# Holding batch 1's input loads behind the last weight conversion, with planner durations and priorities redone

## The chip, the cores and the metric

The kernel runs on one core of a Trainium2 chip. The metric is the device time of one launch in microseconds; the kernel before takes 2090.18 us as the median of three runs (2088.63 to 2092.16).

## The reference, cut to what matters

The input x holds 8 batches of 3072 rows by 256 columns. A two-dimensional Fourier transform (rows, then columns) is taken of each batch and its real part kept. Two dense layers follow, on all 24576 rows:

```
X = fft(fft(x, axis=1), axis=2).real              # 8 x 3072 x 256
h = max(X @ w1, X @ w2, X @ w3);  y = h @ w_out   # 256 -> 768 -> 256
h = y @ w_in                                      # 256 -> 1024
solu = h * softmax(h);  ln = (solu - mean) / sqrt(var + 1e-6) * g_ln
out = ln @ w_out2                                 # 1024 -> 256
```

All weights arrive as 64-bit floats and x as 32-bit floats. The kernel computes in pairs of 16-bit halves (a high and a low part).

## The kernel before, in words

**Two kinds of work.** The weights are prepared once. Each of the 16 weight pieces is loaded as raw 64-bit words (`ld`, SyncE, into one of two `raw` buffers), its magnitude is taken by ScalarE (`ga`, L961), and four VectorE instructions build the 32-bit float (`gd`, L965, L966, L967, L969). The pieces are 768 elements wide (w3, w1, w2 and w_out) or 512 (w_in, then w_out2, whose four are keyed `f`; ("gd", "f", 3) is the last of all). After that come subtractions, small matmuls with the column transform, common power-of-two scales, and the split into halves. The last chain of the preparation is that of w_out2: gains, mean, subtraction on GpSimd, scale, split (`wfg`, `wfm`, `wfs`, `wfn`, `wfh`, `wfl`). When the whole preparation is over, `open` releases its memory to the second layer, and `mh`, `ml` and then the first layer-2 matmul `h` (L802) can follow.

**The stream of x.** Each batch has 4 chunks: a load (`xla`, L387, SyncE, 768 KB, one of two `xs` buffers), a pair sum (`xgh`, L394; on VectorE for batch 0, on GpSimd for all others), a sum and a difference (`xfly`, L433, two instructions, GpSimd), a square sum, a scale, a split (`xlo`, L453 on GpSimd, or L354 on VectorE for half of batch 0), and matmuls (`al`). A batch feeds 6 of the 48 row tiles s; tile s takes transposes `z`, matmuls `be`, layer 1 (`l1`, `rl`, `rh`, `rlo`, `m`), and layer 2 (`h`, `he`, `hv`, `vl`, `vt`, `o`) on 4 subtiles.

**What sets the order.** Nothing is scheduled at run time. A planner in Python (`Schedule.run`, L253) simulates all engines with a duration for each operation and emits each engine's instructions in the order of that simulation. `deps` tell it what must come first; among operations that can start it takes the one with the lowest due time `vt`, which is a base value plus an entry of `BIAS`. Each engine, and the queue of SyncE that issues all loads, then works through its list in order. The semaphores that hold on the chip come from the data that instructions share, not from `deps`: a dep between operations that share no tile changes the emitted order alone. So `deps` at L610 between a load of x and ("gd", "f", 3) leaves no wait of SyncE on VectorE in the program.

**Due times that matter here.** For batch 1 the base value of `xgh` and `xfly` is near 4, and their BIAS is -8.8 and 21.8; that of `rlo` is 97.5 on top of s. On GpSimd they come before `rlo` wherever both can start.

Of the kernel before, what the change touches and what calls it, by code (L numbers as in the profile page):

```python
# [20 lines left out]
NCH = NG // GC  # L21
# [16 lines left out]
BIAS = {("xla", 0): 6.642, ("xgh", 0): 10.341, ("xfly", 0): -9.394, ("xsq", 0): -0.709, ("xhi", 0): 6.403,  # L38
        ("xlo", 0): 17.171, ("al", 0): -2.445, ("ah", 0): -11.543, ("alo", 0): -8.31, ("xnm", 0): -8.319,
        ("et", 0): -11.353, ("eth", 0): -10.064, ("etl", 0): -10.524, ("xall", 0): -24.875, ("xsc", 0): -9.255,  # L40
        ("mu", 0): 3.3, ("xla", 1): 19.575, ("xgh", 1): -8.838, ("xfly", 1): 21.834, ("xsq", 1): 19.306,
        ("xnm", 1): -2.102, ("xhi", 1): 6.849, ("xlo", 1): 2.359, ("al", 1): -2.09, ("ah", 1): 26.235,
        ("alo", 1): -10.133, ("et", 1): -13.32, ("eth", 1): 3.942, ("etl", 1): -8.044, ("xall", 1): -1.555,
        ("xsc", 1): -25.218, ("mu", 1): 3.943, "xla": -20.985, "xgh": 16.273, "xfly": 95.893, "xsq": 148.589,
        "xnm": 34.632, "xhi": -119.918, "xlo": -89.65, "al": -59.029, "ah": -52.388, "alo": -87.057, "et": 0.242,
        "eth": -1.663, "etl": 3.014, "xall": -61.653, "xsc": -117.176, "mu": 56.199, ("zt", 0): -196.624,
# [27 lines left out]
        ("wcn", 1): -20.429, ("wne", 1): 6.325, ("wz", 1): -4.186, ("sub", 2): 7.956, ("wc", 2): 24.519,  # L74
        ("wce", 2): 24.431, ("am", 2): -1.999, ("wcn", 2): 11.089, ("wne", 2): 5.888, ("wz", 2): 1.956, ("amj",): 3.057,
        ("ws", "dg"): -5.917, ("ws", "all"): 1.262, ("ws", "pow"): -4.852, ("wsc", "part"): -14.198, ("wsc",): -1.52,
        ("whi", 1): -3.795, ("wlo", 1): -10.118, ("whi", 2): 23.432, ("wlo", 2): 6.478, ("wl1",): 1.684,
# [5 lines left out]
        ("os3", "dg"): 5.184, ("os3", "all"): 0.493, ("os3", "pow"): -17.762, ("scm", "part"): 12.326, ("scm",): 10.839,  # L83
        ("w3r",): -7.29, ("onm", 0): -0.103, ("ohi", 0): 2.169, ("olo", 0): 9.107, ("onm", 1): -0.381,
        ("ohi", 1): 8.157, ("olo", 1): -36.337, ("w3h",): -11.737, ("w3l",): 7.415, ("ld", "i"): -4.455,
        ("ga", "i"): 9.704, ("gd", "i"): 7.311, ("ami", 0): 4.584, ("wio", 0): -1.893, ("wih", 0): 22.616,
        ("wil", 0): -7.519, ("ami", 1): -0.805, ("wio", 1): 2.701, ("wih", 1): 0.766, ("wil", 1): 3.984,
        ("amij",): 9.396, ("is", "dg"): 13.68, ("is", "all"): 11.251, ("is", "pow"): -9.987, ("isc",): -11.798,
        ("win",): 0.578, ("gl",): -9.399, ("ld", "f"): 1.759, ("ga", "f"): -10.816, ("gd", "f"): -7.915,
        ("wfg", 0): -2.918, ("wfg", 1): 1.353, ("wfg", 2): -26.177, ("wfg", 3): -20.174, ("wfm",): -6.94,  # L90
        ("wfe",): 10.633, ("wfs", 0): 0.706, ("amf", 0): -6.053, ("wfs", 1): -24.272, ("amf", 1): 13.388,
        ("amfj",): 3.48, ("fs", "dg"): -1.106, ("fs", "all"): -5.106, ("fs", "pow"): -7.273, ("wfc", "part"): 9.879,
        ("wfc",): -13.035, ("wfn", 0): 3.542, ("wfh", 0): -6.144, ("wfl", 0): -4.219, ("wfn", 1): -11.469,
        ("wfh", 1): 3.372, ("wfl", 1): 8.053, ("wf",): 0.298, ("open",): -1.093}
# [210 lines left out]
def fft_moe_solu_kernel(ctx, tc, x, x_last, w1, w2, w3, w_out, w_in2, w_out2, g_ln, c_alpha, c_beta, c_w, c_eye, out):  # L305
# [6 lines left out]
    op = sch.op  # L312
# [238 lines left out]
    def is_special(s):  # L551
        return s % NSB == NSB - 1
# [54 lines left out]
    def x_ops(b, c):  # L607
        k = (b, c)
        v = max(NSB * b - 2.0, -1.2) + 0.09 * c
        op(("xla", *k), "SP", 2900, x_load, k, v - 0.5, deps=[("xla", b, c - 1)] if c else [("xla", b - 1, NCH - 1)] * (b > 0),  # L610
           take=["xs"], lag=2500)
        op(("xgh", *k), *(("Pool", 2450) if b else ("DVE", 1100)), x_pairs, (*k, pool if b else dve), v - 0.3, deps=[("xla", *k)])
        op(("xfly", *k), "Pool", 2450, x_fly, k, v - 0.2, deps=[("xgh", *k)], take=["uv"], give=["xs"])
# [440 lines left out]
    for i in (1, 2):  # L1054
# [3 lines left out]
        for a in range(2):  # L1058
            pop(("wc", i, a), "PE", 2900, w_dft, (i, a), v, take=["mh"[a]],
                deps=[("sub", i, 0), ("sub", i, 1), ("const",)] + [("wc", 1, e) for e in range(2) if i > 1])  # L1060
# [277 lines left out]
```

## Time and profile before

| | us |
|---|---|
| median of three runs | 2090.18 |
| the profiled execution | 2085.87 |
| its span, first to last instruction | 2084.1 |
| busy in the span: TensorE | 1976.3 |
| VectorE | 1787.0 |
| ScalarE | 1551.7 |
| GpSimd | 1406.0 |

The profiled execution has its own time, 1.8 us above its span. The engines' busy times are averages over two quite different stretches: the preparation, in which TensorE waits often and at a lower clock, and the long even part. In the profile, PE is TensorE, DVE VectorE, ACT ScalarE, POOL GpSimd, SP SyncE.

### The profile page before, as it was taken

The numbers are of one execution on the slowest core, as the hardware profiler recorded it, in microseconds if no ns is written. First come the engines' busy times: TensorE is split into PE (matmuls) and PEld (weight loads), VectorE is DVE, ScalarE is ACT, GpSimd is POOL, SyncE is SP. The second block draws the span as 40 slices with busy tenths as digits, with TensorE's granted clock in tenths as the row PEclk, the third lists the DMA queues.
The fourth block names the chain that finished last, engine by engine and source line by source line (L and its number), as shares of the span: only waits on it lengthen the run. The fifth ranks groups of instructions, "written<-read, shape, count | busy, mean of one in ns | idle before, by whom it ended". The sixth has DMA issues, their size and how long they took to land. (4 is left out here: it accounts for less than half of the span.)

```text
span 2084.1 us, 41702 instructions
## 1 busy us (share of the span) xinstructions
PE 1976.3 (95%) x15004; PEld 1353.8 (65%) x15004; DVE 1787.0 (86%) x4090; ACT 1551.7 (74%) x3037; POOL 1406.0 (67%) x1814
## 2 busy tenths in 40 slices
PE   4569999999999999999999999999999999999998
PEld 2346666676666666666766666666666666666666
DVE  6989889888888888888888898888888888888884
ACT  2578976777887778777887778877787777777775
POOL 3669975656976679665786668766675656665663
PEclk8669999999999999999999999999999999999999
DMA  7534643333453335523543334533343234233325
GB/s 215 149 75 83 116 82 72 67 67 77 95 114 74 65 78 115 102 57 67 108 102 77 67 77 97 98 77 61 79 75 81 56 73 87 62 80 73 66 48 122
DMA packets 472706, 178.87 MB, mean 86 GB/s; under 512 B 453577, under 2 KB 453802, under 8 KB 469290
## 3 DMA queue, kind: packets, MB, share of 16 engines
q1 hardware_dynamic: 472498, 176.20, 40.4%
q8 instruction: 117, 1.92, 0.4%
q14 instruction: 91, 0.75, 0.1%
HBM read 37.75 MB, written 25.17 MB: 30 GB/s over the span
## 5 line engine op out<-in xcount | busy, mean ns | idle before, releaser
L877 PE MATMUL omm<-wf,vt 128*128 128x256 f16 x4608 | 533.1, 273 | 6.0 <-DMA vt<-vh 5.3
L802 PE MATMUL h<-win,mo 128*128 128x512 f16 x2280 | 523.4, 379 | 2.3 <-DVE v L832 1.8
L877 PEld LDWEIGHTS <-vt 128*128 128x128 f16 x4608 | 450.3, 98 | 73.2 <-DMA vt<-vh 6.6
L680 PE MATMUL l<-pq,wl 128*128 128x256 f16 (+2 forms) x3456 | 453.3, 274 | 23.9 <-DVE sv L714 8.4
L728 POOL TENSOR_TENSOR rhl<-sv,rhl 128x512 f16<-128x512 f32 x288 | 336.8, 1175 | 196.5 <-ACT rhl L723 195.4
L863 POOL TENSOR_TENSOR vh<-v,vh 128x1024 f16<-128x1024 f32 x188 | 401.4, 2135 | 62.0 <-ACT vh L859 61.2
L680 PEld LDWEIGHTS <-wl 128*128 128x128 f16 x3456 | 332.2, 98 | 131.8 <-DVE sv L714 17.9
L738 PE MATMUL m<-rhl,wo 128*128 128x512 f16 x1728 | 413.7, 379 | 1.8 <-POOL rhl L728 1.0
L700 DVE SCALAR_TENSOR_TENSOR l<-ny,wn,l 128x256 f32<-128x256 f32 (+1 forms) x672 | 318.6, 481 | 111.1 <-ACT bs L351 110.3
L802 PEld LDWEIGHTS <-mo 128*128 128x128 f16 x2304 | 221.8, 98 | 249.0 <-DVE v L832 10.2
L351 ACT ACTIVATE bs<-l 128x256 f32<-128x256 f32 (+1 forms) x576 | 216.2, 379 | 158.1 <-PE l L680 138.6
L811 DVE TENSOR_REDUCE hst<-h 128x1 f32<-128x1024 f32 x190 | 231.6, 1219 | 50.8 <-PE h L802 49.8
L832 DVE SCALAR_TENSOR_TENSOR v<-h,hst,e 128x1024 f32<-128x1024 f32 x190 | 243.2, 1280 | 33.2 <-ACT e L826 25.3
L738 PEld LDWEIGHTS <-wo 128*128 128x128 f16 x1728 | 165.4, 99 | 154.0 <-issue 2.9
L837 ACT ACTIVATE jk<-v,hst 128x1024 f16<-128x1024 f32 x192 | 220.0, 1146 | 60.5 <-DVE v L832 59.0
L723 ACT CAST rhl<-sv 128x512 f16<-128x512 f32 x288 | 176.4, 613 | 112.7 <-DVE sv L719 96.4
L826 ACT ACTIVATE e<-h,hst,ms 128x1024 f32<-128x1024 f32 x190 | 228.9, 1205 | 6.3
L859 ACT CAST vh<-v 128x1024 f16<-128x1024 f32 x192 | 198.8, 1035 | 4.7 <-DMA vt<-vh 4.5
L850 POOL TENSOR_SCALAR hst<-hst,sc 128x1 f32<-128x1 f32 x192 | 66.0, 344 | 191.1 <-ACT jk L837 154.1
L719 DVE SCALAR_TENSOR_TENSOR sv<-l,sv 128x512 f32<-128x512 f32 x240 | 164.9, 687 | 3.6
L753 POOL TENSOR_TENSOR mo<-s,mw 128x512 f16<-128x512 f32 x96 | 121.5, 1281 | 12.3 <-ACT mw L351 8.1
L713 DVE SCALAR_TENSOR_TENSOR sv<-l,bs 128x256 f32<-128x256 f32 x288 | 120.5, 418 | 8.5 <-POOL rhl L728 0.6
(168 smaller groups left out, 2583.4 us busy)
## 6 DMA issues: line engine op xcount, KB each, us to landing
xs<-in_x_dram SPq DMA_DIRECT2D x32, 768.0 KB, 6.3
out_dram<-ob SPq DMA_DIRECT2D x96, 256.0 KB, 2.1
raw<-in_w_dram SPq DMA_DIRECT2D x6, 768.0 KB, 7.3
raw<-in_w_out_dram SPq DMA_DIRECT2D x14, 256.0 KB, 2.9
vt<-vh SPq DMA_TRANSPOSE x192, 4.3
raw<-in_w_in_dram SPq DMA_DIRECT2D x4, 512.0 KB, 4.5
cb<-in_c_beta_dram SPq DMA_DIRECT2D x1, 1553.0 KB, 12.9
z<-x SPq DMA_TRANSPOSE x48, 3.4
```

The source lines that it names most:

```text
L351: act.activation(dst, src, AF.Copy, scale=scale)
L680: mm(o, w_[w], hl[:, a, e, c0:c0 + n_], start=(n == 0), stop=(n == 2))
L700: dve.scalar_tensor_tensor(p[:, 0:WA], pq[s][1][:, 0:WA], w, p[:, 0:WA], ALU.mult, ALU.add)
L728: pool.tensor_tensor(t[:, 1], svs.pop((s, j, 0)), t[:, 0], ALU.subtract)
L738: mm(m[:, h], wo[:, w, j, hs], t[:, a], start=(j == 0 and n == 0), stop=(j == NJF - 1 and n == 2))
L802: mm(hp[:, f], m[:, a, d, ts_], win[:, w, d, fs], start=(n == 0), stop=(n == 5))
L811: dve.tensor_reduce(st[:, 0], y["h"], op=ALU.max, axis=AX.XY, negate=True)
L826: act.activation(y["e"], y["h"], AF.Exp, bias=st[:, 11], scale=ms_col(s, MS_T), accum_out=st[:, 3])
L832: dve.scalar_tensor_tensor(y["v"], y["h"], st[:, 2], y["e"], ALU.mult, ALU.mult, accum_out=st[:, 4])
L837: act.activation(new(hpool[0], "jk", [128, 2, 512], F16), y["v"], AF.Square, bias=st[:, 4], scale=-float(FF2), accum_out=st[:, 6])
L863: engine.tensor_tensor(y["vh"][:, 1], y["v"].rearrange("p a b -> p (a b)"), y["vh"][:, 0], ALU.subtract)
L877: mm(y["o"][:, 0:D], vt[:, a * 8 + c], wf[:, w, c], start=(n == 0), stop=(n == 23))
```

## The change

Batch 1's first load of x gets one more dep: the last weight conversion. (Its other chunks and the later batches follow it by the deps that were there.) Some durations that the planner uses are set higher, and all entries of BIAS are new numbers. The tiles, buffers, engines and arithmetic are the same; only the order of instructions on the engines and queues can differ.

```
-BIAS = {("xla", 0): 6.642, ..., ("xla", 1): 19.575, ("xgh", 1): -8.838, ("xfly", 1): 21.834, ... "rlo": 97.526, ...}
+BIAS = {("xla", 0): 3.913, ..., ("xla", 1): 18.196, ("xgh", 1): 5.745, ("xfly", 1): 26.145, ... "rlo": 68.905, ...}
...
-        op(("xla", *k), "SP", 2900, x_load, k, v - 0.5, deps=[("xla", b, c - 1)] if c else [("xla", b - 1, NCH - 1)] * (b > 0),
+        op(("xla", *k), "SP", 3500, x_load, k, v - 0.5, deps=[("xla", b, c - 1)] if c else [("xla", b - 1, NCH - 1)] * (b > 0) + [("gd", "f", 3)] * (b == 1),
...
-            op(("be", *k), "PE", (240, 480)[p], beta_mm, ...)
+            op(("be", *k), "PE", (264, 528)[p], beta_mm, ...)
...
-        op(("l1", *k), "PE", 658, l1_mm, ...)
+        op(("l1", *k), "PE", 663, l1_mm, ...)
...
-        slow, fast = 70 + 1.04 * n, 70 + 0.52 * n
+        slow, fast = 80 + 1.145 * n, 110 + 0.585 * n
...
-        pop(("ld", *key), "SP", 3.6 * n, f64_load, ...)
+        pop(("ld", *key), "SP", 4.4 * n, f64_load, ...)
...
-            pop(("wc", i, a), "PE", 2900, w_dft, ...)
+            pop(("wc", i, a), "PE", 4000, w_dft, ...)
...
-        pop(("wcn", i), "PE", 2340, w_dft_n, ...)
+        pop(("wcn", i), "PE", 3000, w_dft_n, ...)
```

## Rows read from the trace of the kernel before

**Rows 1.** Busy time by stretch (us from the start): engines, granted TensorE clock, DMA
```profile
0.00:57.00 57.00, 25.59 (x70) 15.45 (x70) 36.30 (x40) 18.45 (x30) 22.01 (x21) 0.88 0.75 222
57.00:132.00 75.00, 35.06 (x237) 26.90 (x238) 72.15 (x107) 44.44 (x88) 48.97 (x30) 0.58 0.52 134
132.00:162.00 30.00, 24.43 (x139) 15.79 (x138) 21.93 (x74) 27.73 (x50) 22.16 (x31) 0.91 0.03 6
162.00:200.00 38.00, 35.02 (x317) 23.48 (x315) 35.68 (x84) 31.15 (x65) 36.49 (x31) 1.00 0.39 77
200.00:2000.00 1800.00, 1782.07 (x13713) 1220.65 (x13711) 1571.51 (x3691) 1379.95 (x2719) 1241.31 (x1637) 1.00 0.40 80
2000.00:2084.00 84.00, 74.14 (x535) 51.58 (x533) 49.48 (x100) 49.94 (x90) 35.03 (x67) 0.99 0.47 98
```

**Rows 2.** Timeline of VectorE, TensorE, SyncE's queue: last conversion, first h, last raw load
```profile
130.28 1.46 DVE L969 SCALAR_TENSOR_TENSOR st<-raw,st 128x512 int32<-128x512 int32 x1
...
166.55 2.75 PE L802 MATMUL h<-win,mo 128*128 128x512 f16 x12
...
115.86 0.81 SPq L949 DMA_DIRECT2D raw<-in_w_out_dram  x2
```

**Rows 3.** VectorE's groups by form, 57 to 132 us: count | busy us, mean ns
```profile
L967 DVE SCALAR_TENSOR_TENSOR st<-raw,st 128x512 int32<-128x512 int32 x8 | 8.3, 1043 | 0.1
L969 DVE SCALAR_TENSOR_TENSOR st<-raw,st 128x512 int32<-128x512 int32 x8 | 8.1, 1019 | 0.0
L354 DVE SCALAR_TENSOR_TENSOR wl<-st,sc,wl 128x768 f16<-128x768 f32 x4 | 8.1, 2036 | 0.0
L965 DVE TENSOR_SCALAR st<-st 128x512 f32<-128x512 f32 x8 | 7.3, 918 | 0.3 <-ACT st L961 0.3
L966 DVE TENSOR_SCALAR st<-st 128x512 int32<-128x512 int32 x8 | 7.1, 883 | 0.1
L348 DVE TENSOR_SCALAR am<-am 128x2 int32<-128x2 int32 x1 | 5.1, 5094 | 0.0
...
L969 DVE SCALAR_TENSOR_TENSOR st<-raw,st 128x768 int32<-128x768 int32 x1 | 3.0, 2999 | 0.0
...
L348 DVE TENSOR_SCALAR am<-am 128x1 int32<-128x1 int32 x2 | 0.3, 148 | 0.0
```

**Rows 4.** VectorE's timeline, the same forms while GpSimd stood still
```profile
81.17 0.42 DVE L965 TENSOR_SCALAR st<-st 128x512 f32<-128x512 f32 x1
...
93.93 0.43 DVE L966 TENSOR_SCALAR st<-st 128x512 int32<-128x512 int32 x1
...
96.53 0.68 DVE L969 SCALAR_TENSOR_TENSOR st<-raw,st 128x512 int32<-128x512 int32 x1
...
77.77 1.01 DVE L354 SCALAR_TENSOR_TENSOR wl<-st,sc,wl 128x768 f16<-128x768 f32 x1
...
13.57 0.96 DVE L969 SCALAR_TENSOR_TENSOR st<-raw,st 128x768 int32<-128x768 int32 x1
```

**Rows 5.** Timeline of GpSimd (and of VectorE, last line) around 82 and 100 us
```profile
81.68 3.08 POOL L453 TENSOR_TENSOR uh<-uv,uh 96x1024 f16<-96x1024 f32 x1 [4.59 <-ACT uh L445]
...
100.58 2.47 POOL L433 TENSOR_TENSOR uv<-xs 96x512 f32<-96x512 f32 x2
103.02 2.33 POOL L394 TENSOR_TENSOR xs<-xs 97x1024 f32<-97x1024 f32 x1
...
100.28 5.09 DVE L348 TENSOR_SCALAR am<-am 128x2 int32<-128x2 int32 x1
```

**Rows 6.** GpSimd's instructions on the buffers of x (`xs`) by stretch
```profile
57.00:132.00 75.00, 34.36 (x17) 0.58 0.52 134
132.00:162.00 30.00, 0.00 (x0) 0.91 0.03 6
162.00:200.00 38.00, 9.73 (x6) 1.00 0.39 77
```

**Rows 7.** VectorE's groups by form, 300 to 1900 us
```profile
L719 DVE SCALAR_TENSOR_TENSOR sv<-l,sv 128x512 f32<-128x512 f32 x198 | 136.1, 687 | 3.2
...
L719 DVE SCALAR_TENSOR_TENSOR sv<-sw,sv 128x512 f32<-128x512 f32 x42 | 45.1, 1074 | 0.4
```

More of the change, by code (lines that the diff above doesn't have):

```diff
@@ L37 @@
 HOP = dict(PE=200, DVE=130, ACT=150, Pool=150, SP=60)
[L38 to L46, printed above, removed]
[27 rows of a table removed]
[L74 to L77, printed above, removed]
[5 rows of a table removed]
[L83 to L94, printed above, removed]
@@ new lines @@
+BIAS = {("xla", 0): 3.913, ("xgh", 0): 34.799, ("xfly", 0): -38.007, ("xsq", 0): 23.212, ("xhi", 0): 11.929,
+        ("xlo", 0): 23.876, ("al", 0): -18.632, ("ah", 0): -15.284, ("alo", 0): -0.968, ("xnm", 0): -32.17,
+        ("et", 0): -26.116, ("eth", 0): 6.781, ("etl", 0): -39.996, ("xall", 0): -19.961, ("xsc", 0): -35.177,
+        ("mu", 0): -37.967, ("xla", 1): 18.196, ("xgh", 1): 5.745, ("xfly", 1): 26.145, ("xsq", 1): -7.37,
+        ("xnm", 1): -26.645, ("xhi", 1): 18.119, ("xlo", 1): -12.788, ("al", 1): 0.024, ("ah", 1): -1.903,
+        ("alo", 1): -22.945, ("et", 1): -10.243, ("eth", 1): -0.308, ("etl", 1): 10.347, ("xall", 1): 3.52,
+        ("xsc", 1): -18.909, ("mu", 1): 8.834, "xla": -35.206, "xgh": 9.507, "xfly": 99.83, "xsq": 147.293,
+        "xnm": 31.691, "xhi": -116.418, "xlo": -86.305, "al": -61.683, "ah": -46.137, "alo": -92.537, "et": 0.016,
+        "eth": 2.854, "etl": 7.849, "xall": -51.5, "xsc": -118.594, "mu": 63.532, ("zt", 0): -203.637,
[24 rows of a table added]
+        ("const",): -23.518, ("eye",): 9.596, ("constb",): 5.976, ("ld", 0): -25.93, ("ga", 0): 34.626,
+        ("gd", 0): -11.561, ("ld", 1): -21.531, ("ga", 1): -7.482, ("gd", 1): 23.214, ("ld", 2): -6.687,
+        ("ga", 2): 16.553, ("gd", 2): 24.091, ("sub", 1): -12.102, ("wc", 1): 7.152, ("wce", 1): -1.677,
+        ("am", 1): 38.371, ("wcn", 1): -37.192, ("wne", 1): 33.251, ("wz", 1): 13.049, ("sub", 2): 49.742,
+        ("wc", 2): 11.471, ("wce", 2): 24.6, ("am", 2): 1.444, ("wcn", 2): -13.165, ("wne", 2): -9.829,
+        ("wz", 2): -2.18, ("amj",): 3.147, ("ws", "dg"): -1.65, ("ws", "all"): -11.251, ("ws", "pow"): 12.944,
+        ("wsc", "part"): -39.515, ("wsc",): 3.261, ("whi", 1): -2.03, ("wlo", 1): -0.692, ("whi", 2): 25.704,
[6 rows of a table added]
+        ("scm", "part"): 27.744, ("scm",): -5.484, ("w3r",): -1.376, ("onm", 0): -7.27, ("ohi", 0): -30.766,
+        ("olo", 0): 26.373, ("onm", 1): -11.059, ("ohi", 1): 3.742, ("olo", 1): -59.531, ("w3h",): -18.86,
+        ("w3l",): 28.542, ("ld", "i"): 20.066, ("ga", "i"): 23.016, ("gd", "i"): 3.272, ("ami", 0): 10.252,
+        ("wio", 0): 19.512, ("wih", 0): 45.094, ("wil", 0): -11.125, ("ami", 1): -5.753, ("wio", 1): 2.627,
+        ("wih", 1): 36.889, ("wil", 1): 5.236, ("amij",): 15.29, ("is", "dg"): 8.763, ("is", "all"): 35.379,
+        ("is", "pow"): -10.409, ("isc",): -21.646, ("win",): 6.927, ("gl",): 2.71, ("ld", "f"): 34.252,
+        ("ga", "f"): -14.274, ("gd", "f"): -16.632, ("wfg", 0): 17.273, ("wfg", 1): -2.77, ("wfg", 2): -50.255,
+        ("wfg", 3): -28.967, ("wfm",): -9.849, ("wfe",): 5.167, ("wfs", 0): -27.207, ("amf", 0): -41.7,
+        ("wfs", 1): -28.19, ("amf", 1): 6.448, ("amfj",): 9.143, ("fs", "dg"): -24.677, ("fs", "all"): -3.746,
+        ("fs", "pow"): 0.738, ("wfc", "part"): 35.922, ("wfc",): -17.908, ("wfn", 0): -7.146, ("wfh", 0): -14.354,
+        ("wfl", 0): -21.968, ("wfn", 1): -33.02, ("wfh", 1): 43.4, ("wfl", 1): 6.051, ("wf",): 8.178, ("open",): -3.712}
@@ L650, in fft_moe_solu_kernel @@
             before = [("be", s, 0)] if p else [("be", s - 1, 1)] if s else []
-            op(("be", *k), "PE", (240, 480)[p], beta_mm, k, v, deps=[("zt", s), ("constb",), *before] + [("etl", b)] * is_special(s),
+            op(("be", *k), "PE", (264, 528)[p], beta_mm, k, v, deps=[("zt", s), ("constb",), *before] + [("etl", b)] * is_special(s),
                take=["misc"] if p else ["misc", "pq"])
@@ L755, in l1_ops @@
     def l1_ops(k, v, deps):
-        op(("l1", *k), "PE", 658, l1_mm, k, v, deps=[("bl", k[0], 0), ("bl", k[0], 1)] + deps, take=["l1"])
+        op(("l1", *k), "PE", 663, l1_mm, k, v, deps=[("bl", k[0], 0), ("bl", k[0], 1)] + deps, take=["l1"])
         op(("l1b", *k), "ACT", 265, l1_b, k, v, deps=[("l1", *k)], take=["bs"])
@@ L973, in from_f64 @@
     def from_f64(key, srcs, dst, n, v, take=(), after=()):
-        pop(("ld", *key), "SP", 3.6 * n, f64_load, (key, srcs, n), v - 0.2, deps=after, take=["raw", *take], lag=2000)
+        pop(("ld", *key), "SP", 4.4 * n, f64_load, (key, srcs, n), v - 0.2, deps=after, take=["raw", *take], lag=2000)
         magnitude, parts = f64_parts(key, dst, n)
@@ L1058, in fft_moe_solu_kernel @@
         for a in range(2):
-            pop(("wc", i, a), "PE", 2900, w_dft, (i, a), v, take=["mh"[a]],
+            pop(("wc", i, a), "PE", 4000, w_dft, (i, a), v, take=["mh"[a]],
                 deps=[("sub", i, 0), ("sub", i, 1), ("const",)] + [("wc", 1, e) for e in range(2) if i > 1])
@@ L1063, in fft_moe_solu_kernel @@
             pop(("am", i, a), "DVE", 870, amax, (2 * i - 2 + a, lambda i=i, a=a: wrs[i, a]), v, deps=[("wce", i, a)])
-        pop(("wcn", i), "PE", 2340, w_dft_n, (i,), v, deps=[("wce", i, 1)], take=["misc"])
+        pop(("wcn", i), "PE", 3000, w_dft_n, (i,), v, deps=[("wce", i, 1)], take=["misc"])
         pop(("wne", i), "ACT", 56, w_evac_n, (i,), v, deps=[("wcn", i)], give=["misc"])
```

62 rows, old and new, of the table BIAS are left out of this document.

## The prediction, made before the kernel was run

> **What bounds the kernel now.** I read the busy times by stretch first [rows 1]. From 200 to 2000 us TensorE is busy 1782.07 of 1800, at full clock. So this part is bound by TensorE, its whole slack is 17.9 us, and the same matmuls run after the change. The last 84 us hold 9.9 us of TensorE's idle time. The first 200 us are another matter: TensorE is busy 25.6 + 35.1 + 24.4 + 35.0 = 120.1 us of 200, and from 57 to 132 us its granted clock is 0.58. A startup shorter by some amount moves everything behind it forward by as much, because what follows is a full TensorE.
>
> So I asked which engine fills the startup. From 57 to 132 us it is VectorE, 72.15 of 75 us; TensorE has 35, ScalarE 44, GpSimd 49 [rows 1]. The last conversion's last instruction ends at 130.28 + 1.46 = 131.7 us, and the first h matmul starts at 166.55 [rows 2]. From 132 to 162 us no engine is full (VectorE 21.9 of 30, GpSimd 22.2, ScalarE 27.7): this stage is a chain, the tail of w_out2's preparation beside layer 1 of the first row tiles.
>
> Next I asked whether VectorE's 72 us are work, by its groups by form [rows 3] against single instructions of the same form while GpSimd stood still [rows 4]. They are not: the same conversion step takes 0.9 to 1.0 us in the mean and 0.42 to 0.68 when alone. The clearest case is a two-element mask that starts at 100.28 and takes 5.09 us: GpSimd had started a pair of x instructions at 100.58 and another at 103.02, which ends at 103.02 + 2.33 = 105.35, and the mask ends at 105.37 [rows 5]. VectorE's instruction ends where GpSimd's run of instructions ends. GpSimd worked 34.36 us on x buffers in this stretch [rows 6], and all of it belongs to batches 1 and 2, since batch 0 takes its pair sums on VectorE and its last sums of the other kind are done before 57 us.
>
> **The change part by part.**
>
> The dep. It moves batch 1's loads, and with them their sums on GpSimd, in the planned order behind the last conversion; batch 2 goes behind batch 1. What leaves the stretch is the excess of VectorE's instructions. L967: 8 x (1043 - 680) ns = 2.9 us, taking L969's clean 0.68 for both. L969: 8 x (1019 - 680) = 2.7. L354 on wl: 4 x (2036 - 1010) = 4.1. L965: 8 x (918 - 420) = 4.0. L966: 8 x (883 - 430) = 3.6. The mask L348: 5094 - 148 = 4.9. The 768-wide L969: 2999 - 960 = 2.0. Sum 24.2 us [rows 3, 4]. Not all of it goes, as some of GpSimd's work in the stretch is not that of batches 1 and 2. Batch 0's split at 81.68 lasts 3.08 us and stays [rows 5]; a VectorE instruction behind it loses between nothing and 3.1 us, and I take 1.6. The last conversion step lies beside the weights' own subtractions and took 1.46 instead of 0.68 us [rows 2, 4]; I count 0.8 for it and as much for a neighbour, 1.6 in all. So 24.2 - 1.6 - 1.6 = 21.0 us go, with bounds 24.2 - 3.1 - 1.6 = 19.5 and 24.2.
>
> What is late next. VectorE stands still for 75 - 72.15 = 2.85 us of this stretch [rows 1]. With faster conversions the two raw buffers and ScalarE's step in front come nearer to the limit, so I double the idle time: 2.8 us are given back, with bounds 0 and 5.6. The last conversion would then end near 113.5 us instead of 131.7.
>
> What the moved work meets. A chunk takes GpSimd 9.73 / 2 = 4.9 us undisturbed (six instructions are two chunks) [rows 6], a batch 19.5 us. It now falls into the chain behind the conversions, where GpSimd also has the subtractions of the weights and of layer 1's halves. GpSimd is idle there for 30 - 22.16 = 7.8 us [rows 1]. If a whole batch had to go through before the first h, 19.5 - 7.8 = 11.7 us would be added to the chain; if the planner finds only gaps, nothing. Batch 1 isn't needed until row tile 6, so the lower bound is the nearer one: I take one chunk in front of something on the path, 4.9 us.
>
> Does this work disturb VectorE later? The instruction with one input in PSUM takes 687 ns; the same with both in SBUF takes 1074 [rows 7]. Only the special row tiles, one in six, have the slow form, so 6 instructions per batch: 6 x 0.39 = 2.3 us on an engine that has 228 us of slack in 1800 [rows 1]. I take 0, at most 2.3. The Trainium skill, SBUF — State Buffer, "Who interferes with whom", says that VectorE contends with GpSimd in its two-port modes or with two SBUF inputs, and that whichever starts first holds the shared ports for its whole instruction. By that rule the excess is exchanged, not removed, wherever x's sums meet such forms again; rows 7 show how few remain, so the sum by the rule would be 2.3 us worse at most.
>
> The durations. They change nothing on the chip by themselves. They let the planned order of the startup lie nearer to what happens: the new 110 + 0.585 x 512 = 410 and 80 + 1.145 x 512 = 666 ns are the clean 0.42 and 0.68 us [rows 4]. Gain or loss from this alone: bounded by TensorE's idle time between 132 and 200 us, 5.6 + 3.0 = 8.6 us [rows 1], in either direction; I take 0.
>
> The priorities. For the even part and the end they can win at most 17.9 and 9.9 us [rows 1], and lose as much if the new order is looser. l1 and be get durations up by 1% and 10%, which isn't much for an order to follow. I take 0, with 5 us either way for the range.
>
> SyncE's queue. Nothing waits on a semaphore for the conversion: the loads only stand further back. Behind them in the list are the transposes z and vt. The loads wait for free x buffers alone, which are long empty by then, so I cost this at 0; if a load did stand in front of a transpose, it would cost its own issue, under 1 us as for the raw loads [rows 2].
>
> Sum: 21.0 - 2.8 - 4.9 = 13.3 us less. The profiled execution would go from 2085.87 to 2072.6. The median of the runs shown is 4.3 us higher, at 2090.18, and on it I forecast 2076.9 us.
>
> **The rivals.**
>
> 1. The chain that remains eats the gain. The first h is held by the last preparation as well as by layer 1 of tile 0. If the 30 us stage grows by the full 11.7 us and the idle time by 5.6, then 21.0 - 17.3 = 3.7 us remain: 2086.5, hardly to be told from no change. For it: GpSimd has 36.49 of 38 us from 162 to 200 [rows 1]. Against it: TensorE was near full there all the same, and there is no hurry for batch 1.
>
> 2. It doesn't do what it says. Without a semaphore, SyncE issues a load of batch 1 as soon as the queue lets it. The last raw load goes out at 115.86, 16 us ahead of the last conversion's end [rows 2], so x's sums may still meet the last two conversions: two of the eight 512-wide ones, 2 x (0.36 + 0.34 + 0.50 + 0.45) = 3.3 us of the gain lost, and 2080 comes out. Against more than this: GpSimd's list is ordered too. This lies inside my range.
>
> 3. Slower: GpSimd becomes the bound of the ramp. By its due times x's sums go ahead of rlo. Were batches 1 and 2 both to pass before the first h is fed, that is 39 us, less 7.8 idle, less the 18.2 us (21.0 - 2.8) won ahead: 13 us later, 2103. It decides at the first h: later than 166.55 us, and the change loses. For it: the two batches have only been delayed, not spread. Against it: batch 2's sums need buffers that batch 1 frees late, and the planner counts these durations.
>
> 4. The even part loosens under the new priorities: TensorE's idle time there goes from 17.9 to 28 us and the result is 2087, about no change.
>
> 5. More comes out: the bounds at their best, 24.2 us, plus 5 of the 8.6 us in the ramp: 29 us, 2061.
>
> **How the numbers follow.** The forecast with rival 2 in it: 0.56, its own range 2068 to 2083 (giving back 0 or 11.7 instead of 4.9, conversion bounds, 5 us for the priorities, not all at once). Rival 1: 0.12. Rival 3: 0.14. Rival 4: 0.10. Rival 5: 0.08. A measurement can tell 0.2%, 4.2 us, from no change. Faster: 0.56 + 0.08, with a third each of rivals 1 and 4 (0.07): 0.71. Slower: 0.14 and a little of rival 4: 0.16. Same: 0.13. The range runs from 2062 to 2093: it leaves out most of rival 3 and half of rival 5, less than 2 in 10.
>
> **What would show it.** In the profile after: no x instruction of batch 1 on GpSimd before the last conversions; L965 to L969 of 512 near 0.42 and 0.68 us in the mean, and no mask of 5 us; the last conversion's end near 113 us; first h between 145 and 158 us; TensorE's idle time in the even part near 18 us. Wrong would be: clean conversions with a first h still near 166 (the chain was not VectorE's), or an early h with the gain lost behind 200 us (GpSimd or the priorities).

## The result, and the profile after

The changed kernel takes 2116.82 us (median; 2112.44 to 2118.45) against 2089.40 (2088.13 to 2092.16) of the kernel before in the same session: a ratio of 1.0128, 95% interval 1.0115 to 1.0140. It is 27 us slower, outside the range; I had forecast 13 us faster. The profiled execution took 2117.41 us, its span is 2115.6, which is 31.5 us above the span of before (the two profiled executions lie further apart than the medians).

First the startup, which is where I looked. VectorE's groups by form, 57 to 125 us of the changed kernel (count | busy us, mean ns | idle before), to be read against [rows 3]:

```profile
L969 DVE SCALAR_TENSOR_TENSOR st<-raw,st 128x512 int32<-128x512 int32 x8 | 6.3, 782 | 0.0
L965 DVE TENSOR_SCALAR st<-st 128x512 f32<-128x512 f32 x8 | 5.6, 699 | 2.6 <-ACT st L961 2.6
L967 DVE SCALAR_TENSOR_TENSOR st<-raw,st 128x512 int32<-128x512 int32 x8 | 5.5, 689 | 0.1
L966 DVE TENSOR_SCALAR st<-st 128x512 int32<-128x512 int32 x8 | 5.3, 664 | 0.1
L354 DVE SCALAR_TENSOR_TENSOR wl<-st,sc,wl 128x768 f16<-128x768 f32 x4 | 3.9, 1008 | 0.0
...
L348 DVE TENSOR_SCALAR am<-am 128x2 int32<-128x2 int32 x1 | 0.2, 163 | 0.0
```

The mask that took 5.09 us takes 0.16, the 768-wide halves 1.01 instead of 2.04. No x instruction of batch 1 or later stands beside the conversions any more, as it should be: the last of them ends at 122.4 us and GpSimd's first instruction on batch 1 starts at 126.80. The timelines of VectorE, TensorE and SyncE's queue answer to [rows 2]:

```profile
121.73 0.69 DVE L969 SCALAR_TENSOR_TENSOR st<-raw,st 128x512 int32<-128x512 int32 x1
...
158.09 3.86 PE L802 MATMUL h<-win,mo 128*128 128x512 f16 x12
...
109.22 0.43 SPq L387 DMA_DIRECT2D xs<-in_x_dram  x1
```

The last conversion ends at 122.4 us (131.7 before), the first h starts at 158.1 (166.55), batch 1's first load of x goes out at 109.2. So the first h comes 8.5 us earlier, and the kernel is still slower. The busy times by stretch (columns as in [rows 1]) show where that went:

```profile
0.00:57.00 57.00, 24.58 (x68) 14.66 (x68) 38.57 (x37) 16.96 (x27) 22.33 (x21) 0.88 0.67 211
57.00:132.00 75.00, 51.48 (x315) 37.56 (x316) 59.04 (x143) 52.88 (x106) 29.38 (x31) 0.66 0.38 92
132.00:162.00 30.00, 19.02 (x116) 10.83 (x115) 19.92 (x50) 18.29 (x36) 27.10 (x23) 0.83 0.21 53
162.00:200.00 38.00, 32.33 (x221) 20.48 (x222) 28.85 (x71) 29.96 (x53) 33.27 (x31) 0.96 0.42 94
200.00:2000.00 1800.00, 1760.92 (x13567) 1203.15 (x13567) 1546.20 (x3651) 1368.21 (x2693) 1238.05 (x1611) 1.00 0.39 80
2000.00:2115.60 115.60, 105.09 (x719) 70.57 (x717) 69.16 (x141) 68.90 (x125) 56.88 (x100) 0.97 0.43 89
```

Busy time alone misleads while the clock is low, so I multiply it by the granted clock, which gives the matmul work done in microseconds at full clock (the granted clock of a stretch is the mean over its two levels, 1.2 and 2.4 GHz, as a share of 2.4). From 57 to 132 us that is 51.48 x 0.66 = 34.0 against 35.06 x 0.58 = 20.3 before: 13.6 us ahead. From 132 to 200 it is 15.8 + 31.0 = 46.8 against 22.2 + 35.0 = 57.3: 10.4 of them are given back in 68 us. The same product from 200 to 300 us is 8.2 lower (TensorE busy 93.30 at 0.98, against 99.66 at 1.00). In the even part TensorE's idle time from 400 to 2000 us has doubled; before and after, columns as above:

```profile
400.00:2000.00 1600.00, 1584.42 (x12206) 1085.82 (x12205) 1395.56 (x3275) 1222.84 (x2408) 1094.62 (x1444) 1.00 0.39 79
```

```profile
400.00:2000.00 1600.00, 1567.61 (x12067) 1072.15 (x12066) 1375.49 (x3246) 1209.32 (x2382) 1082.15 (x1421) 1.00 0.39 79
```

15.6 us of idle time became 32.4, and after the longer gaps the clock falls too (0.97 from 1300 to 1400 us). By counts of the finished l, m, h and o matmuls the changed kernel is about 5 us behind at 400 us and 27 behind at 2000. So some 22 us are lost in the even part, and some 5 net in a startup that had been 13.6 ahead. The other 4 of the 31.5 us between the two spans lie behind 2000 us, where the granted clock is 0.97 against 0.99.

What the even part waits for shows in the waits of the changed kernel from 400 to 2000 us (us in total, times, longest), first ScalarE's, then those of SyncE's queue:

```profile
ACT vh L859 <- DMA vt<-vh: 84.9, 61, 3.0
```

```profile
SPq L868 <- PE omm L877: 960.5, 131, 16.8
```

Before, the first of these is not there at all, and the second is this:

```profile
SPq L868 <- PE omm L877: 208.6, 39, 17.8
```

A transposing DMA reads one of two vh buffers and fills one of three vt buffers, and a vt buffer is free only when its o matmul is through. If o comes late in the order, the transposes back up, vh stays full, and ScalarE, which works its list in order, stands before the next vh with the `bs` copies of layer 1 behind it.

And in the ramp, the timeline of the changed kernel around TensorE's longest gap there (start, us, engine, line, operation, tiles; in brackets the idle time before it and what ended it):

```profile
137.93 3.71 POOL L433 TENSOR_TENSOR uv<-xs 97x512 f32<-97x512 f32 x3
...
141.70 0.10 POOL L399 MEMSET xb<- 32x4 f32 x1
141.83 1.06 ACT L403 ACTIVATE zj<-uv 97x1024 bf16<-97x1024 f32 x1 [2.06 <-POOL xb L399]
...
142.88 0.64 ACT L351 ACTIVATE bs<-l 128x256 f32<-128x256 f32 x2
143.28 0.88 DVE L700 SCALAR_TENSOR_TENSOR l<-ny,wn,l 128x256 f32<-128x256 f32 x2 [3.53 <-ACT bs L351]
...
144.88 1.04 PE L680 MATMUL l<-pq,wl 128*128 128x256 f16 x4 [4.87 <-DVE sv L714]
```

Read from the bottom: TensorE waits 4.87 us for VectorE, VectorE 3.53 for ScalarE's `bs`, and `bs` stands behind the square of batch 1's x (L403), which waits for a small instruction of GpSimd (L399) that stands behind the sums of that x in GpSimd's list. Work that nobody needs until row tile 6 is in front of layer 1 on an engine that keeps its order.

### The profile page after: what moved, and what is told of

Its sections match the earlier page's. It is cut to its first block, busy times and chain, and to the rows that moved or that the text cites. A ratio compares the mean times of both kernels' runs of the same rounds, so it can differ in the third digit from the quotient of the medians.

```text
span 2115.6 us, 41733 instructions
## 1 busy us (share of the span) xinstructions
PE 1993.4 (94%) x15004; PEld 1357.3 (64%) x15004; DVE 1761.7 (83%) x4090; ACT 1555.2 (74%) x3037; POOL 1407.0 (67%) x1814
## 4 chain that ended last, share of the span: by engine, by line
PE 64%; DVE 16%; ACT 7%; DMA 5%; POOL 4%; issue 4%; SPq 0%; DVEq 0%; ACTq 0%; POOLq 0%
PE h L802 18%; PE omm L877 17%; PE l L680 14%; PE m L738 12%; DMA vt<-vh 3%; DVE v L832 2%; DVE hst L811 2%; DVE l L700 2%; DVE sv L719 2%; ACT e L826 1%; PE beta L569 1%; ACT bs L351 1%; POOL uh L453 1%; POOL vh L863 1%; DVE sv L714 1%
## 5 line engine op out<-in xcount | busy, mean ns | idle before, releaser
L877 PE MATMUL omm<-wf,vt 128*128 128x256 f16 x4608 | 536.5, 274 | 10.4 <-DMA vt<-vh 6.0
L802 PE MATMUL h<-win,mo 128*128 128x512 f16 x2280 | 526.3, 381 | 12.0 <-DVE v L832 11.8
L680 PE MATMUL l<-pq,wl 128*128 128x256 f16 (+2 forms) x3456 | 455.1, 275 | 40.2 <-DVE sv L714 18.3
L802 PEld LDWEIGHTS <-mo 128*128 128x128 f16 x2304 | 222.6, 98 | 261.5 <-DVE v L832 21.0
L351 ACT ACTIVATE bs<-l 128x256 f32<-128x256 f32 (+1 forms) x576 | 213.4, 379 | 121.2 <-PE l L680 112.7
L859 ACT CAST vh<-v 128x1024 f16<-128x1024 f32 x192 | 200.0, 1042 | 87.6 <-DMA vt<-vh 84.9
L753 POOL TENSOR_TENSOR mo<-s,mw 128x512 f16<-128x512 f32 x96 | 122.2, 1279 | 28.6 <-ACT mw L351 27.0
```

Of the source, the lines that this page charges most:

```text
L351: act.activation(dst, src, AF.Copy, scale=scale)
L680: mm(o, w_[w], hl[:, a, e, c0:c0 + n_], start=(n == 0), stop=(n == 2))
L802: mm(hp[:, f], m[:, a, d, ts_], win[:, w, d, fs], start=(n == 0), stop=(n == 5))
L877: mm(y["o"][:, 0:D], vt[:, a * 8 + c], wf[:, w, c], start=(n == 0), stop=(n == 23))
```

## The experiments

Thirteen kernels, each timed beside the kernel before, whose median lies between 2089.48 and 2089.75 us in these sessions; the ratios are to that. Where a run fixes the order, the planner's loop is replaced by a list of the same operations, and only the list differs; in those kernels all lines below the planner have numbers 38 lower (L802 is L764, L859 is L821).

```
     def run(self):
-        ...                      # picks the next operation by deps, durations and BIAS
+        for i in ORDER:          # a written-out list of the same operations
+            o = self.ops[keys[i]]
+            o.fn(*o.args)
```

| run | us | ratio, 95% interval | last conversion ends | first h | idle 400 to 2000 |
|---|---|---|---|---|---|
| before | 2089.40 | | 131.7 | 166.6 | 15.6 |
| the change | 2116.82 | 1.0115 to 1.0140 | 122.4 | 158.1 | 32.4 |
| e1 new start, old even part | 2096.18 | 1.0020 to 1.0044 | 121.2 | 157.1 | 16.9 |
| e2 old start, new even part | 2116.61 | 1.0118 to 1.0148 | 131.2 | 166.9 | 30.9 |
| e3 wait and durations | 2118.99 | 1.0126 to 1.0156 | 118.3 | 171.2 | 32.0 |
| e4 x later by 80 us | 2117.35 | 1.0121 to 1.0155 | 109.9 | 143.5 | 23.0 |
| e5 the change, 3 vh | 2105.05 | 1.0052 to 1.0086 | 121.9 | 157.7 | 20.0 |
| e6 wait alone | 2110.23 | 1.0082 to 1.0112 | 102.8 | 182.5 | 18.7 |
| e7 durations alone | 2112.06 | 1.0093 to 1.0123 | 142.8 | 183.1 | 20.9 |
| e8 x on VectorE | 2096.59 | 1.0019 to 1.0045 | 121.8 | 164.6 | 17.4 |
| e9 later x held back | 2081.86 | 0.9949 to 0.9978 | 121.6 | 157.2 | 18.3 |
| e10 new start, held back | 2101.68 | 1.0043 to 1.0073 | 122.1 | 156.1 | 21.4 |
| e11 priorities alone | 2172.70 | 1.0380 to 1.0411 | 133.7 | 182.1 | 58.3 |
| e12 hold alone | 2086.35 | 0.9975 to 0.9993 | 125.7 | 160.4 | 16.9 |
| e13 spread alone | 2089.26 | 0.9992 to 1.0010 | 125.1 | 160.4 | 17.0 |

The last column is the time in us for which TensorE is not busy from 400 to 2000 us. Times by stretch and idle times are from each run's profiled execution.

**Which stretch loses.** Theory A: the new order of the even part is looser and loses 22 of the 27 us. Theory B: x coming later disturbs the even part by itself.

e1 takes the change's order up to 300 us of the plan and the order of before from there:

```
-ORDER = order of before
+ORDER = [operations the change starts before 300 us] + [the others in the order of before]
```

> The changed kernel's order up to 300 us of the plan, the order of the kernel before from there on; the same instructions. Theory A (the new priorities make the order of the even part looser, 22 of the 27 us; the startup costs some 5): the even part's TensorE idle time is back near 16 us from 400 to 2000, and the time is about 2089 + 6 = 2095, between 2090 and 2100. Theory B (loading x later is itself what disturbs the even part, whatever the priorities): still above 2108.

e2 is the reverse, cut at 200 us:

```
+ORDER = [operations before starts before 200 us] + [the others in the order of the change]
```

> The mirror image: the order of the kernel before up to 200 us of the plan, the changed kernel's order from there on. Theory A: the startup is that of before and the even part has 30 us or more of TensorE idle time from 400 to 2000, 2107 to 2118 us. Theory B: x was loaded early, so the even part is as before, 2089 to 2096.

e1's row from 400 to 2000 us (columns as above):

```profile
400.00:2000.00 1600.00, 1583.11 (x12209) 1086.04 (x12207) 1394.18 (x3274) 1220.55 (x2405) 1092.01 (x1435) 1.00 0.39 80
```

and e2's:

```profile
400.00:2000.00 1600.00, 1569.08 (x12062) 1072.39 (x12061) 1375.21 (x3244) 1207.36 (x2380) 1079.03 (x1419) 1.00 0.38 79
```

With the old order behind it, the same start loses 6.7 us instead of 27 (2096.18), and TensorE's idle time is back at 16.9. With the old start and the new order behind it everything is lost again (2116.61, idle 30.9), and the waits at vh are there (83.6 us). Theory A holds: some 20 us are the order of the even part, some 7 the start. The two don't add exactly: with the old start, the new order from 200 us of the plan on costs the whole 27.

**Which edit makes the order loose.** e3 keeps the wait and the new durations, with the old priorities:

```
-BIAS = {new numbers}
+BIAS = {numbers of before}
```

> The changed kernel with the old BIAS: the new dep and the new durations stay. Theory A: the even part's idle time is that of before, near 16 us; the startup is ordered by priorities that were made for other durations and may lose up to 20 us: 2090 to 2110, and a first h later than the changed kernel's 158 us. Theory B: as slow as the changed kernel in the even part (30 us idle), 2110 or more in all.

It is as slow as the change (2118.99, idle 32.0), without the waits at vh (2.8 us, once). So the new priorities are not needed for a loose even part, which is not what A said, and the vh buffers are not the only way to one; what loosens this one was not found. The three edits then each by themselves: the wait,

```
-... [("xla", b - 1, NCH - 1)] * (b > 0)
+... [("xla", b - 1, NCH - 1)] * (b > 0) + [("gd", "f", 3)] * (b == 1)
```

> The added wait alone: the planner keeps the old durations and the old priorities. Theory A (any plan that is worked out anew from 100 us on has a looser even part than the one from before, whatever triggered it): TensorE idle in 400 to 2000 us 25 to 35 against 15.6 before, 2105 to 2125 us. Rival (the new durations or the new priorities loosen it): idle 15 to 18, and only the start counts, 2085 to 2100. The conversions should end at 113 to 123 us in either case.

the durations (70 + 1.04 n to 80 + 1.145 n, and the others of the diff),

> The new durations alone: old priorities, no added wait, so x of batch 1 is loaded at 52 to 81 us as before. Theory A: even part as loose as with the change, idle 25 to 35 us in 400 to 2000, and the conversions as slow as before (end at 128 to 136 us), so 2110 to 2130. Rival (durations that follow the trace do the plan good or nothing, as the prediction had it at 0): 2084 to 2094, idle 14 to 18.

and the priorities:

```
-BIAS = {numbers of before}
+BIAS = {new numbers}
```

> The new priorities alone, with the old durations and without the wait. Theory P (the tight vh buffers of the changed kernel come with the new priorities, since neither the wait nor the durations alone showed them): ScalarE's wait at vh for the transposing DMA over 50 us in the run, TensorE idle in 400 to 2000 us 27 to 34, 2105 to 2130. Rival (it takes the priorities together with the durations): idle 15 to 22 and that wait under 10 us; 2088 to 2110 by what its start does.

The wait alone leaves the even part nearly as it was (idle 18.7), and the durations add 5 us of idle time to it (20.9), where theory A asked for 25 to 35: in the form "any new plan is looser" it has fallen. Each still costs some 20 us, more than the rival theories allowed, and much of it in the start: by busy time times clock e6 is 19.5 us behind the kernel before at 400 us, e7 13.3. With the wait alone the conversions end at 102.8 us, 29 us earlier than before and earlier than I expected, and the first h comes 16 us later than before, because the total of batch 1's x stands in TensorE's own list in front of the chain (TensorE's timeline of e6):

```profile
148.16 0.59 PE L407 MATMUL total<-xb,unit 128*128 128x4 f32 x2 [20.00 <-ACT zj L403]
```

The priorities alone cost 83 us and are the loosest of all (row of e11 from 400 to 2000 us):

```profile
400.00:2000.00 1600.00, 1541.67 (x11777) 1053.15 (x11776) 1331.86 (x3174) 1186.33 (x2331) 1055.31 (x1394) 0.99 0.38 77
```

My expectation there named the vh buffers and was wrong in that: ScalarE's wait at them is 19.6 us, and the longest TensorE gaps are o matmuls that wait for their transposed tile (28.8 us in four gaps). The effects don't add: 21 + 23 + 83 us alone, 27 together. The new priorities do far worse with the old durations and without the wait (83 us) than with both (27). But the whole set is no better than the wait alone or the durations alone, and all four mixtures that were run, like the set itself, are slower than before.

**What the vh buffers are worth.** e5 is the change's order, with one number changed:

```
-                vh=2, vt=3, ob=2, ...
+                vh=3, vt=3, ob=2, ...
```

> The change's order to the instruction, but with three buffers for the fp16 pair of V (vh) instead of two. In the change's trace ScalarE waits 84.9 us (61 times) at the vh buffers for a transposing DMA, and the DMA queue waits 960 us for o matmuls that free the transposed buffers; neither wait is in the trace of before. Theory V (these waits are where the even part loses): with a third buffer the ScalarE wait falls under 20 us, TensorE's idle time in 400 to 2000 us falls from 32.4 to 17 to 22, and the time to 2100 to 2106 us. Rival (the waits are a sign of a late TensorE and not its cause; what idles it is the order in which VectorE and ScalarE serve it): the ScalarE wait falls, the idle time stays at 28 to 34, and the time at 2112 to 2119.

```profile
ACT vh L821 <- DMA vt<-vh: 0.5, 1, 0.5
```

```profile
400.00:2000.00 1600.00, 1579.99 (x12160) 1083.75 (x12159) 1383.87 (x3268) 1213.86 (x2391) 1087.76 (x1432) 1.00 0.39 79
```

The wait of 84.9 us is gone (first row, the waits of e5; second row, its stretch), idle time falls from 32.4 to 20.0 and the time by 11.8 us. SyncE's queue waits for the o matmuls as long as before the edit (949.7 us); the third buffer only keeps that from reaching ScalarE. So 12 of the some 20 to 22 us that the even part lost are this chain. What the rest is was not taken apart.

**Where the start's gain went.** e4 takes the order of before and moves only the x steps of batch 1 and later, those before 480 us of the plan, up to 80 us back:

> The order of the kernel before, in which nothing but the stream of x from batch 1 on (loads, sums, splits, alpha matmuls, z transposes) stands 80 us of the plan later, until it meets the old place again near 480 us. This is the dep's idea without new durations or priorities. The forecast's own step (contention with the conversions is worth 13 to 21 us at the end): 2068 to 2078, conversion steps of 512 near 0.42 and 0.68 us, first h near 148 us. Rival (the startup's length is not set by VectorE's conversions, or the gain is lost in the ramp): 2085 to 2095. Theory B: 2105 or more.

```profile
200.00:300.00 100.00, 88.63 (x694) 59.28 (x692) 73.18 (x179) 70.90 (x138) 71.05 (x75) 0.97 0.39 84
300.00:400.00 100.00, 86.36 (x623) 56.71 (x622) 78.24 (x182) 72.75 (x140) 70.70 (x102) 0.98 0.39 85
```

The first h comes at 143.5 us, 23 us earlier than before, and 25 us of TensorE's time are lost from 200 to 400 us (its rows above), where by the plan batch 1's steps now press against row tile 6; no run took that apart. Theory B has the time right (2105 or more) and not the place: from 600 to 2000 us, behind the moved steps, TensorE idles 13.4 us against 12.7 before. So the first h decides nothing by itself.

e8 puts the pair sums and the residuals of batch 1's x on VectorE, with the change's planner, and the order of before from 250 us:

```
-... (("Pool", 2450) if b else ("DVE", 1100)), x_pairs, (*k, pool if b else dve)
+... (("Pool", 2450) if b > 1 else ("DVE", 1100)), x_pairs, (*k, pool if b > 1 else dve)
...
-            pool.tensor_tensor(t[:, 1], xuv.pop((b, c)), t[:, 0], ALU.subtract)
+            (dve if b == 1 else pool).tensor_tensor(t[:, 1], xuv.pop((b, c)), t[:, 0], ALU.subtract)
```

> The change with two of the four GpSimd steps of batch 1's x (the pair sums and the residuals, 18 of its 36 us of GpSimd work) on VectorE, planned with the change's numbers; from 250 us of the plan on, the order of before. Theory (after the change GpSimd is the bound of the ramp, 15.7 of 18 and 23.0 of 25 us in 132 to 175 us, because batch 1's x now stands among rlo, wfs and wfl): first h at 150 to 160 us, TensorE busy in 132 to 162 us over 22 (19.0 with the change), and 2082 to 2094 us, that is 3 to 14 under the 2096.2 of the change's start with the old order behind it. Rival (the ramp loses by TensorE's low clock and by the split of VectorE, which gets 9 us more work): 2093 to 2100.

2096.59, no better than e1; the first h goes to 164.6, and GpSimd fills up with other x (29.55 us on x's buffers from 132 to 200 us against 26.51 in e1). That points to whose x it is. GpSimd's busy time on x's buffers by stretch shows 52.5 us from 132 to 300 us in the changed kernel, more than two batches, where [rows 6] and the same view of before to 300 us have 29.2:

```profile
132.00:162.00 30.00, 14.13 (x9) 0.83 0.21 53
162.00:200.00 38.00, 11.49 (x9) 0.96 0.42 94
200.00:300.00 100.00, 26.84 (x17) 0.98 0.52 113
```

From 57 to 300 us it is 54.8 us (34 instructions) in the changed kernel and 63.6 (35) in the kernel before, and a batch is 12 such instructions, 19.5 us by the prediction's count: both work on x of batches 2 and 3 in the first 300 us, as soon as buffers allow, though batch 2 is first needed for row tile 12. e9 holds that back in the order of before and spreads batch 1's chunks:

```
 ORDER = order of before
+  x steps of batches 2 to 4 (loads, sums, squares, splits): 280 us and later, before 103 to 260
+  x steps of batch 1: the same sequence, further apart
```

> The order of before, neither the change's wait nor its numbers, with one thing moved: the early steps of x for batches 2 to 4, which the kernel before does at 103 to 260 us on GpSimd, are held back to 280 us and later, and batch 1's chunks are spread further apart; the other steps keep their order. Theory H (what disturbs the start is that x of batches that aren't needed for hundreds of us takes GpSimd, first beside the conversions, then in the ramp; batch 1 alone fits): last conversion ends at 116 to 124 us (131.7 before), first h at 150 to 160, TensorE busy in 132 to 200 us over 61 (59.4 before, 51.4 with the change), even part as before (idle 14 to 19 in 400 to 2000), 2072 to 2084 us. Rival B (moving x to a later place costs as much as it brings, as when batch 1 was moved by 80 us): TensorE idle grows in 300 to 500 us instead, and 2088 to 2105.

```profile
57.00:132.00 75.00, 43.42 (x276) 33.52 (x277) 64.09 (x118) 54.66 (x108) 41.73 (x33) 0.64 0.43 105
132.00:162.00 30.00, 23.71 (x163) 14.49 (x162) 26.19 (x80) 22.72 (x42) 23.09 (x27) 0.94 0.00 1
162.00:200.00 38.00, 37.62 (x342) 25.98 (x341) 36.12 (x86) 32.83 (x67) 25.98 (x27) 1.00 0.29 56
200.00:300.00 100.00, 99.91 (x737) 67.89 (x735) 85.47 (x202) 73.53 (x146) 65.43 (x81) 1.00 0.49 96
300.00:400.00 100.00, 95.09 (x713) 63.83 (x714) 89.49 (x214) 76.80 (x152) 80.94 (x108) 1.00 0.47 95
```

2081.86 us: the first version that beats both kernels, by 7.9 us against before. Theory H holds for its times (last conversion 121.6, first h 157.2, TensorE 61.3 us busy from 132 to 200), and TensorE stays full from 200 to 300 us, where the change lost 6.7. Some 3 us are paid back from 300 to 400, where the held x now lies.

The two moves apart, and the same hold behind the change's start:

> The run that beat both kernels (2081.9 us) moved two things in the order of before. Here the early x of batches 2 to 4 alone is held back to 280 us and later; batch 1's steps stand as before. Theory H2 (x of the later batches is most of it: it leaves GpSimd at 103 to 121 us beside the conversions, and altogether in 160 to 280 us): last conversion ends at 124 to 128 us, first h at 160 to 164, and 2083 to 2087 us. Rival S (batch 1's chunks were the ones in the way, the later batches sat in gaps): last conversion 129 to 132, first h 165 to 168, 2087 to 2092.

> The other half: batch 1's chunks are spread as in the run with 2081.9 us, and x of batches 2 to 4 comes as early as before. Theory H2: last conversion 126 to 131 us, first h 161 to 167, 2086 to 2091 us. Rival S: last conversion 119 to 124, first h 155 to 160, 2080 to 2085.

> The change's start (as in the run that put the old order behind it, 2096.2 us), with x of batches 2 to 4 held back to 240 us and later, and the order of before behind 300 us of the plan. Theory H: GpSimd's x work in 132 to 300 us falls from 52 to under 35 us, and the time to 2084 to 2092. Rival C (batch 1 by itself is too late behind the last conversion: its square on ScalarE and its sums stand in front of layer 1 in the ramp): TensorE busy in 132 to 200 us stays at 50 to 53, and 2093 to 2100.

The hold alone wins 3.2 us (interval 0.07 to 0.25%), the spread alone nothing that can be told. Both bring the first h to 160.4, 6 us earlier than before. From 162 to 200 us they part (first row the hold alone, second the spread alone):

```profile
162.00:200.00 38.00, 37.27 (x317) 25.24 (x316) 35.61 (x83) 29.15 (x57) 24.20 (x28) 0.99 0.31 50
162.00:200.00 38.00, 34.63 (x273) 21.91 (x271) 31.34 (x74) 28.87 (x56) 33.58 (x29) 0.91 0.37 77
```

With the hold, TensorE's work there (busy by clock) is 37.27 x 0.99 = 36.9; with the spread alone it is 34.63 x 0.91 = 31.5, and the early h is given back. GpSimd works 9.73 us on x there with the spread alone and none with the hold, which is the likely reason. Together the two win 7.9, more than the sum, so theory H2, by which the hold is most of the gain, has the times of each half about right and not the share. Behind the change's start the hold takes GpSimd's x work from 132 to 300 us down to 27.7 us, as expected, and gains nothing: 2101.68, 5.5 above e1, of which 4.5 are idle time in the even part (21.4 against 16.9). TensorE is busy 53.2 us from 132 to 200, about what rival C expected. Its list also has some of batch 1's own steps in other places than e1's (its squares and scalings on ScalarE, some up to 40 places later), so this is not a test of the later batches alone. It speaks against them as what the change's start suffers from, and for batch 1 itself behind the conversions, in the lists of ScalarE and GpSimd, as in the gap before 144.88 us. That is a reading of the trace; no run took batch 1 out of that place alone.

## Why the prediction was wrong, point by point

- **The reading of the startup** held: VectorE's conversions were slowed by GpSimd, and mostly clean once x had gone. Of the 24.2 us that I summed for the seven groups, 5.0 remain (L965 8 x 0.28, L966 8 x 0.23, L969 8 x 0.10, L967 0.1), so 19.2 went; I had taken 21.0 with 19.5 as the lower bound.
- **What is late next** was mis-sized. Up to the last conversion's end VectorE is busy 54.58 of 65.4 us, so it idles 10.8 us where it had idled 2.85: 8.0 given back, not 2.8, and outside the bound of 5.6. Some 2 us of other work also moved in front of it, as VectorE's busy time up to there fell by 17.3 us and not by 19.2. The conversion ended at 122.4 instead of 113.5.
- **What the moved work meets**: I put one chunk, 4.9 us, on the path, with 11.7 as the bound. The path lost more than the 13.6 us of work won ahead: at 400 us the sum of busy time by clock is 3.9 us below before. I priced x by GpSimd's idle time. But the price was paid in the lists of ScalarE (the square in front of `bs`) and, in e6, of TensorE (its total, 20 us). And where TensorE has gaps, its clock stays down: 0.83 from 132 to 162 us against 0.91, the h matmul at 158.09 taking 3.86 us against 2.75.
- **Later disturbance of VectorE** I took as 0, at most 2.3 us. Means agree: the two-SBUF form takes 1109 ns (42 of them) against 1074. A single one is another matter; in the changed kernel:

```profile
1547.47 2.96 DVE L719 SCALAR_TENSOR_TENSOR sv<-sw,sv 128x512 f32<-128x512 f32 x1
```

```profile
1546.38 1.28 POOL L753 TENSOR_TENSOR mo<-s,mw 128x512 f16<-128x512 f32 x1
1547.61 2.27 POOL L728 TENSOR_TENSOR rhl<-sv,rhl 128x512 f16<-128x512 f32 x2
```

```profile
1550.81 1.36 PE L680 MATMUL l<-pq,wl 128*128 128x256 f16 x11 [2.31 <-DVE pq L354]
```

  VectorE's instruction starts while GpSimd's L753 runs, GpSimd's pair behind that runs to 1549.88, VectorE's instruction ends 0.55 us after it, and TensorE waits 2.31 us for the step behind it. VectorE got through only after all three of GpSimd's instructions. The Trainium skill, SBUF — State Buffer, "Who interferes with whom", has the shared ports as an exclusive lock; these rows agree.
- **The durations at 0, with 8.6 us as the bound** and **the priorities at 0, with 5 us either way**: these two terms are the step that failed most. The edits cost 22.6 and 83 us alone, and the order that came of all three loses some 22 us in the even part, where I had at most 5. I had bounded a loss by a symmetric guess, with no row behind it. The 17.9 us of slack in [rows 1] limits what an order can win; it says nothing of what one can lose. Rival 4 had the mechanism with 10 us of extra idle time and 0.10; from 200 to 2000 us it was 21 (17.9 to 39.1), and it came on top of a startup that won nothing.
- **A number I left unread:** the planner simulates the whole kernel before anything is launched. With the numbers of before its plan ends at 1998.5 us, with those of the change at 2030.5, with the priorities alone at 2082.2. (These are what `Schedule.run` computes for each kernel.) Of the 32 us between the first two, 12.6 are TensorE's longer planned durations and 19.4 its idle time, 16.6 of them before 400 us of the plan. So the plan warned of the start. Of the even part's loss it had 2 us for the change, and 45 for the priorities alone.
- **SyncE's queue at 0**: x's buffers were not "long empty"; from 100 to 200 us the queue stands 42.1 us at x's loads until GpSimd frees them. It cost nothing there, as the first transpose goes out at 173.57 us, when its source is just done (173.55). But in the even part its transposes wait 960 us for o matmuls, and that reaches ScalarE. I had looked at the queue for loads in front of transposes, not for buffers behind them.
- Rival 1, the chain that eats the gain, describes the start as the runs show it, and was too mild: e1, which has only the start, is 6.7 us slower than before. Rival 2 fell: GpSimd's first x instruction of batch 1 came 4 us behind the last conversion. Rival 5 fell with the gain.
- Rival 3 named the ramp and GpSimd, with a first h later than 166.55 us as its sign. The ramp did take the gain, with a first h at 158. The sign was the wrong one; e4 shows a first h at 143 in a kernel 28 us slower.

## What to carry to other kernels

In a kernel whose order is written ahead and whose engines keep it, a bound on what an order can win is no bound on what it can lose: price a new order by running it, and read first where the planner's own simulation ends. Don't use priorities with durations and deps that they weren't made for (83 us here), and where only the start is to change, change the start's list alone: the change's start in front of the old order cost 6.7 us and not 27. Before delaying what is needed soon, look for what comes far too early: here x of batches 2 to 4, held back, gave 3.2 us alone and 7.9 with batch 1 spread, while the wait for batch 1 lost time in every form that was run.

## What the runs showed of the hardware

The same twelve h matmuls take 2.75 us at full clock and 3.86 to 4.45 in the ramp of the changed kernel, at 158.09 and 166.31 us, behind gaps of TensorE; the granted clock from 150 to 175 us is 0.86. Earlier work that leaves gaps therefore brings less than its busy time says: TensorE's busy time over the whole run is 17.1 us higher (1993.4 against 1976.3) for the same matmuls. I had not expected that in a stretch that is ahead.
